# Two woven layers on one core: stores of the turned features on ScalarE's queue, and the last block's feature steps at another pace

## The chip, the core and the metric

The kernel runs on one core of a Trainium2 chip. The core has five engines that each work through their own instructions in order: TensorE (PE in the profile, with PEld for its weight loads), VectorE (DVE), ScalarE (ACT), GpSimdE (POOL) and SyncE (SP). An engine waits for another by semaphores. Transfers (DMAs) are begun by an instruction in the queue of SP or of ScalarE and are then carried out by 16 DMA engines; the instruction that begins one waits, in its queue, for the data that it sends. The metric is the time on the device in microseconds, the median of the runs.

## What is computed

An input x of 2048 rows and 576 columns in fp32 goes through two pairs of layers: linear attention with a learned feature map (32 heads of 18 columns), then an MLP with a squared ReLU and 4608 hidden units. Both use the same weights in both pairs.

```python
def attend(x):                       # on the layer norm of x
    q, k, v = heads(x @ wqkv)
    pq, pk = q @ w_phi, k @ w_phi    # one 18x18 matrix a head
    phi = lambda p: concat([softmax(p), softmax(-p)])
    kv = einsum("bhsf,bhsd->bhfd", phi(pk), v)
    z = einsum("bhsf->bhf", phi(pk))
    num = einsum("bhqf,bhfd->bhqd", phi(pq), kv)
    den = einsum("bhqf,bhf->bhq", phi(pq), z) + 1e-6
    return merge(num / den) @ wo

def mlp(x):                          # on the layer norm of x
    h = relu(x @ w1 + b1)
    return (h * h) @ w2 + b2

for _ in range(2):
    x = x + attend(layernorm(x))
    x = x + mlp(layernorm(x))
```

## The kernel before

Each fp32 operand of a matrix product is split in two parts that TensorE takes at full speed, and a product is three products (high by high, low by high, high by low). The rounding to the high part is ScalarE's work, the difference VectorE's and GpSimdE's.

The 2048 rows are four blocks of 512 rows, and a block is four tiles of 128 rows (t = 0 to 3). The MLP's 4608 hidden units are 36 groups of 128. A group is: the loads of its weights on SP (m_2r, the columns of w1 at L1159 and L244, the rows of w2 at L1161); their rounding on ScalarE (m_2h at L1167, m_2s at L1168 and L1169); the first products on TensorE (m_2ph, 14 matmuls at L1190); Relu and two squares on ScalarE (m_2hr, m_2hb at L1197 to L1199); the second products (m_2acc at L1217 and L1208), which TensorE takes one group behind the first ones. The digit in such a name is the block: m_2 is the MLP of block 2. The trace leaves out the layer, so a_0 and m_0 can be of either.

A layer has an order of its blocks, [3, 2, 0, 1] in the first and [1, 0, 3, 2] in the second. The MLP of order[0] (m_3, then m_1) is woven with the attention of order[1] and with the queries and features of order[2]. The MLP of order[1] (m_2, about 510 to 750 us; m_0, about 1700 to 1950 us) is woven with the rest of order[2]'s attention, then with the whole attention of order[3] (a_1 in the first layer, a_2 in the second), then with the prelude of a pair of MLPs that order[2] and order[3] go through together.

The order of the instructions is set as the program is written, by `weave`: after each step of the MLP (a group has 1 such step) the other side gets `rate` units, and each of its steps costs the units that it names. A smaller cost or a higher rate puts the step earlier. Nothing is sorted later: what is written behind another instruction of the same engine stands behind it in its queue. `held` also places a step behind the MLP's latest square and its low part.

The change touches the features of a block, `g_features`, once each for order[1] and order[2] in `back_first` and for order[3] in `back_second`. Its four tiles go through a pipeline of steps: the parts of the softmax, its exponential, its sums and the products with z, the factors, the scaling, and `turn`. In a round each tile that is under way takes one step, the later steps first, and one more tile begins. `turn` transposes a tile of 128 rows and 1152 columns in squares of 32 on VectorE (L897) and then begins four stores of 144 KB to device memory (a_1ft<-a_1Q1e: block 1, tile 1; L900). When all sixteen stores of a block have landed, `g_out` loads the turned features back (a_1w, L928, in five pieces: 126, 72, 126, 126 and 126 rows), ScalarE rounds each half of a piece (a_1fh, L941), VectorE makes the low part (a_1fl, L942), and TensorE multiplies them (a_1pn, L964). The attention's result is added to x on GpSimdE (L1051) and stored by SP (xm, L1052).

All transfers that SP and ScalarE begin take turns on eight semaphores (DMAHW0 to DMAHW7 in the rows below). A transfer waits in its queue until the one before it on its semaphore has landed.

Of the kernel before, what the change touches and what calls it, by code (L numbers as in the profile page):

```python
# [21 lines left out]
def layers_kernel(  # L22
# [18 lines left out]
    nc = tc.nc  # L41
# [60 lines left out]
    def drain(gen):  # L102
        for _ in gen:
            pass

    def weave(main, other, rate, behind=None):

        due = 0.0
        for _ in main:
            due += rate  # L110
            while due >= 1.0:
                cost = next(other, other)
                if cost is other:
                    break
                due -= cost or 1.0
        with tc.issue_after(dense[behind]) if behind else nullcontext():
            drain(other)

    def pipeline(n, stages, costs):

        for i in range(n + len(stages) - 1):
            for k in reversed(range(len(stages))):
                if 0 <= i - k < n:
                    stages[k](i - k)
                    yield costs[k]

    def paced(gen, cost):
        for own in gen:
            yield own if cost is None else cost
# [510 lines left out]
    def soft_parts(src, name, apart=False):  # L640
        if apart:
            e = sb.tile([P, 2 * D], F32R, tag="hb", name=f"{name}e").bitcast(F32)
            e = e.rearrange("p (s d) -> p s d", s=2)
        else:
            e = sb.tile([P, 2, D], F32, tag="E", name=f"{name}e", bufs=4)
        v = src.rearrange("p (h d) -> p h d", d=DH)
        mm = sb.tile([P, 2, H], F32, tag="mm", name=f"{name}m")
        nc.vector.tensor_reduce(mm[:, 0], v, op=ALU.max, axis=AX.X)
        nc.vector.tensor_reduce(mm[:, 1], v, op=ALU.min, axis=AX.X)
        e4 = e.rearrange("p s (h d) -> p s h d", d=DH)  # L650
        m = mm.unsqueeze(3).to_broadcast([P, 2, H, DH])
        dense["parted"] = nc.vector.tensor_sub(e4[:, 0], v, m[:, 0])
        dense["parted", 1] = nc.gpsimd.tensor_sub(e4[:, 1], m[:, 1], v)
        return e

    def soft_exp(e):
        return nc.scalar.activation(e, e, AF.Exp)

    def soft_sums(e, name):
        r = sb.tile([P, 2, H], F32, tag="r", name=f"{name}r", bufs=4)  # L660
        nc.vector.tensor_reduce(r, e.rearrange("p s (h d) -> p s h d", d=DH), op=ALU.add, axis=AX.X)
        nc.vector.reciprocal(r, r)
        return r
# [142 lines left out]
    def held(gen, keys=("last",)):  # L806

        while True:
            with ExitStack() as behind:
                for key in keys:  # L810
                    behind.enter_context(tc.issue_after(dense[key].ins))
                cost = next(gen, gen)
            if cost is gen:
                return
            yield cost
# [15 lines left out]
    def phi_products(layer, e, name):  # L831
        zb = sums[layer]["zb"]
        ms = [sb.tile([P, D], F32, tag="qk", name=f"{name}{s}", bufs=5) for s in range(2)]
        for s in range(2):
            (nc.gpsimd if s else nc.vector).tensor_mul(ms[s], e[:, s], zb[:, s])
        return ms
# [13 lines left out]
    def phi_scale(e, r, which=(0, 1)):  # L850
        for s in which:
            e3 = e[:, s].rearrange("p (h d) -> p h d", d=DH)
            dense[f"scaled{s}"] = (nc.gpsimd if s else nc.vector).tensor_mul(
                e3, e3, r[:, s].unsqueeze(2).to_broadcast([P, H, DH]))
# [21 lines left out]

        return product, total, factors, scale

    def g_features(layer, raws, ph, name):

        rs, ms = {}, {}

        def start(t):
            ph.append(soft_parts(raws[t], f"{name}Q{t}"))

        def add(t):
            rs[t] = soft_sums(ph[t], f"{name}Q{t}")
            ms[t] = phi_products(layer, ph[t], f"{name}m{t}")

        def factors(t):  # L890
            phi_factors(phi_sums(ms.pop(t), f"{name}u{t}"), rs[t])

        turned[name] = home = dram.tile([2 * D, TB], F32, name=f"{name}ft")

        def turn(t):
            flat = ph[t].rearrange("p s d -> p (s d)")
            nc.vector.transpose(flat, flat)  # L897
            for i in range(NQ):
                at = t * P + 32 * i
                nc.sync.dma_start(home[:, at : at + 32].rearrange("(j f) r -> f j r", f=32),  # L900
                                  flat[32 * i : 32 * i + 32].rearrange("f (j r) -> f j r", r=32))

        yield from held(pipeline(NT, (start, lambda t: soft_exp(ph[t]), add, factors, lambda t: phi_scale(ph[t], rs[t]),
                                      turn), (2.6, 0.4, 3.0, 2.8, 1.2, 1.6)), ("last", "squared"))

    def g_out(layer, b, ph, dst, name, parts=1, pause=None, behind=None, norm=None, mid=None, costs=(None, None), o_first=None):

# [790 lines left out]
            return x  # L1698
        return get

    def g_attend(layer, b, x, raws, dst, name, behind=None, norm=None, mid=(None, None), ph=None):

        if ph is None:
            ph = []
            if raws is None:
                raws = []
                yield from g_queries(layer, b, x, raws, name)
            yield from g_features(layer, raws, ph, name)
        yield 5.0
        if mid[0]:  # L1710
            yield from mid[0]
        yield from g_out(layer, b, ph, dst, name, behind=behind and (behind["last"],), norm=norm, mid=mid[1],
                         costs=(1.0, None if norm else 3.0))
# [108 lines left out]
    for b in range(NB - 1):  # L1822
        norm = g_norm(load_x(b + 1), xT[b + 1], f"n0_{b + 1}")
# [7 lines left out]
    order = [NB - 1, NB - 2] + list(range(NB - 2))  # L1831
    b, prev = order[0], order[1]
    x, xprev = xT[b], xT[prev]
    for layer in range(2):
        ready, raws = barrier(layer, b, prev, x, xprev, kes, vpair, qpair)
        spare["tags"] = []
        early, operands, rows, nxt, keep = [], {}, [], {}, {}
# [7 lines left out]
        def back_second():  # L1845
            yield from g_attend(layer, order[2], None, None, operands, f"a{layer}_{order[2]}", None,
                                g_norm_first, ph=early)
            yield from g_attend(layer, order[3], None, None, operands, f"a{layer}_{order[3]}", None,
                                lambda *a: held(g_norm_second(*a), ("last", "squared")))
            yield from paced(held(prelude, ("last", "squared")), 2.0)  # L1850

        def rows_of(b):
# [75 lines left out]
        back = chained(back_second())  # L1928
# [2 lines left out]
            drain(back)  # L1931
            next(products)

        weave(g_mlp(layer, order[1], nxt, [], f"m{layer}_{order[1]}", None, then), back, 5.0)
        back = iter(()) if layer else chained(back_keys(), True)
        for k, _ in enumerate(products):
            if k == NP - 1:
# [6 lines left out]
        if layer == 0:  # L1944

            prev, b = order[-2], order[-1]
            spare["tags"] = ["acc0", "acc1", "acc2", "acc3", "h"]
            x, xprev, vpair = {}, keep["x"], keep["v"]
# [14 lines left out]
            order = [b, prev] + order[:2]  # L1963
# [22 lines left out]
```

## Time and profile before

| | |
|---|---|
| median of three runs (2436.8, 2439.97, 2958.45) | 2439.97 us |
| the profiled execution | 2442.47 us |
| its span | 2440.8 us |
| TensorE busy | 2412.5 us, 99% |
| VectorE busy | 1560.7 us, 64% |
| ScalarE busy | 1290.9 us, 53% |
| GpSimdE busy | 939.9 us, 39% |
| stores of turned features, number of issues | 96, all on SP |

The shares are averages over stages that differ, so they don't say where a change counts. What matters is where TensorE stands still, and what it then waits for. In the rows of SP the times are those of the instruction that begins a transfer, not of the transfer. A time in brackets behind a row is how long the engine was idle before it, and what ended that.

### The profile page before, as it was taken

Reading aid. Unit: us, or ns where it says so; the run is one execution under the profiler, and the core shown is the slowest. Engines: PE = TensorE matmul, PEld = TensorE weight load, DVE = VectorE, ACT = ScalarE, POOL = GpSimd, SP = SyncE. Lnnn points to the kernel's source line nnn. Section 1 sums busy time; section 2 is a strip of 40 time slices with the busy share of each in tenths; the row PEclk is TensorE's granted clock in tenths of the full one; section 3 lists DMA queues with packets and bytes.
Section 4 is the critical chain, followed back from the end, with each engine's and each line's share of the span. In section 5 each row is a group of like instructions: output and inputs, shape, how many; then the busy total and the mean of one; then the engine's idle time right before and its main releaser. Section 6 shows DMA issues by size and latency. Waiting matters only on the chain. (4 is left out here: it accounts for less than half of the span.)

```text
span 2440.8 us, 41473 instructions
## 1 busy us (share of the span) xinstructions
PE 2412.5 (99%) x14806; PEld 2140.8 (88%) x14806; DVE 1560.7 (64%) x2537; ACT 1290.9 (53%) x2543; POOL 939.9 (39%) x1121
## 2 busy tenths in 40 slices
PE   9999999999999999999999999999998999999999
PEld 8999888888788888888999988888887888888898
DVE  7778848664866655545766788486557675555443
ACT  4344555444446766664433445554455466676643
POOL 4555303222326565542433442032122455565321
PEclk9999999999999999999999999999999999999999
DMA  9124573756654533338753156637667444333364
GB/s 338 64 84 164 163 194 102 168 185 228 151 159 129 162 105 108 112 102 301 254 188 147 59 167 145 173 96 195 194 224 162 130 143 144 119 103 117 110 199 130
DMA packets 370646, 379.40 MB, mean 155 GB/s; under 512 B 142886, under 2 KB 270790, under 8 KB 367878
## 3 DMA queue, kind: packets, MB, share of 16 engines
q1 hardware_dynamic: 369180, 375.37, 51.3%
q8 instruction: 116, 1.90, 0.3%
q10 hardware_dynamic: 1258, 1.37, 0.2%
q14 instruction: 92, 0.75, 0.1%
HBM read 297.22 MB, written 79.41 MB: 154 GB/s over the span
## 5 line engine op out<-in xcount | busy, mean ns | idle before, releaser
L1508 POOL TENSOR_TENSOR m_ps<-m_pr,m_ps 128x128 fp32r<-128x128 f32 x144 | 98.8, 686 | 338.1 <-ACT m_ps L1506 310.9
L1507 DVE TENSOR_TENSOR m_ps<-m_pr,m_ps 128x448 fp32r<-128x448 f32 x144 | 99.8, 693 | 176.1 <-ACT m_ps L1505 176.0
L1550 PE MATMUL m_pacc<-m_ps,m_phb 128*128 128x448 f32 x864 | 185.6, 363 | 0.0
L1550 PEld LDWEIGHTS m_pacc<-m_ps,m_phb 128*128 128x128 f32 x864 | 161.9, 188 | 15.1
L1550 PE MATMUL m_pacacc<-m_ps,m_phc 128*128 128x448 f32 x648 | 147.1, 365 | 0.0
L1505 ACT ACTIVATE m_ps<-m_pr 128x448 fp32r<-128x448 f32 x144 | 82.8, 575 | 115.8 <-issue 66.6
L1550 PEld LDWEIGHTS m_pacacc<-m_ps,m_phc 128*128 128x128 f32 x648 | 119.2, 188 | 7.7
L1190 PE MATMUL m_2ph<-a_2nh,m_2h 128*128 128x512 f32 (+1 forms) x380 | 98.1, 385 | 1.9 <-ACT m_2h L1167 1.7
L1190 PE MATMUL m_0ph<-a_0nh,m_0h 128*128 128x512 f32 (+1 forms) x380 | 97.6, 383 | 1.8 <-ACT m_0h L1167 1.7
L1217 PE MATMUL m_2acc<-m_2s,m_2hb 128*128 128x448 f32 x432 | 95.4, 368 | 2.9 <-ACT m_2s L1168 2.6
L1217 PE MATMUL m_0acc<-m_0s,m_0hb 128*128 128x448 f32 x432 | 95.2, 368 | 2.9 <-ACT m_0s L1168 2.6
L1190 PE MATMUL m_1ph<-t1onh,m_1h 128*128 128x512 f32 (+1 forms) x380 | 95.8, 381 | 0.5 <-ACT m_1hr L1197 0.3
L1190 PE MATMUL m_3ph<-t0onh,m_3h 128*128 128x512 f32 (+1 forms) x380 | 95.7, 381 | 0.2 <-DVE t0onh L534 0.2
L1217 PE MATMUL m_3acc<-m_3s,m_3hb 128*128 128x448 f32 x432 | 93.6, 363 | 0.0
L1217 PE MATMUL m_1acc<-m_1s,m_1hb 128*128 128x448 f32 x432 | 93.5, 363 | 0.0
L1217 PEld LDWEIGHTS m_2acc<-m_2s,m_2hb 128*128 128x128 f32 x432 | 82.0, 191 | 11.7 <-ACT m_2s L1168 3.0
L1217 PEld LDWEIGHTS m_0acc<-m_0s,m_0hb 128*128 128x128 f32 x432 | 81.7, 190 | 11.6 <-ACT m_0s L1168 3.0
L1217 PEld LDWEIGHTS m_3acc<-m_3s,m_3hb 128*128 128x128 f32 x432 | 80.7, 188 | 7.9 <-DVE m_3hb L1200 0.4
L1217 PEld LDWEIGHTS m_1acc<-m_1s,m_1hb 128*128 128x128 f32 x432 | 80.7, 188 | 7.8 <-DVE m_1hb L1200 0.3
L1175 POOL TENSOR_TENSOR m_3s<-m_3r,m_3s 128x128 fp32r<-128x128 f32 x36 | 22.3, 620 | 158.2 <-ACT m_3s L1169 147.0
L1175 POOL TENSOR_TENSOR m_1s<-m_1r,m_1s 128x128 fp32r<-128x128 f32 x36 | 22.0, 612 | 156.7 <-ACT m_1s L1169 139.4
L1190 PEld LDWEIGHTS m_1ph<-t1onh,m_1h 128*128 128x128 f32 x380 | 68.8, 188 | 15.3 <-ACT m_1hr L1197 0.7
(2464 smaller groups left out, 7241.0 us busy)
## 6 DMA issues: line engine op xcount, KB each, us to landing
m_pr<-in_B_w SPq DMA_DIRECT2D x144, 288.0 KB
m_pr<-in_B_w SPq DMA_DIRECT2D x72, 256.0 KB
hd<-m_pu SPq DMA_DIRECT2D x72, 256.0 KB
m_pg<-hd SPq DMA_DIRECT2D x72, 256.0 KB
m_3r<-in_B_w SPq DMA_DIRECT2D x36, 288.0 KB
m_2r<-in_B_w SPq DMA_DIRECT2D x36, 288.0 KB
m_1r<-in_B_w SPq DMA_DIRECT2D x36, 288.0 KB
m_0r<-in_B_w SPq DMA_DIRECT2D x36, 288.0 KB
```

What stands on the lines that cost most here:

```text
L1175: nc.gpsimd.tensor_sub(s2[:, FC + P : FC + 2 * P], r2[:, R:], s2[:, FC : FC + P].bitcast(F32))
L1190: dense["hidden"] = nc.tensor.matmul(ph[:, cols], a, m, start=(k == 0), stop=(k == len(ops) - 1))
L1217: nc.tensor.matmul(acc[t][:, :R], a[:, rows], m, start=(f == 0 and k == 0), stop=(f == NF - 1 and k == 2))
L1505: nc.scalar.activation(s2[:, RO : RO + R], r2[:, :R], AF.Copy)
L1507: nc.vector.tensor_sub(s2[:, RO + R : RO + 2 * R], r2[:, :R], s2[:, RO : RO + R].bitcast(F32))
L1508: nc.gpsimd.tensor_sub(s2[:, FC + P : FC + 2 * P], r2[:, R:], s2[:, FC : FC + P].bitcast(F32))
L1550: nc.tensor.matmul(accs[b][t][:, :R], a[:, rows], m, start=(g == 0 and k == 0), stop=(g == NF - 1 and k == 2))
```

## The change

The four stores of a tile are taken out of `turn` and become a step of their own, `store`, which comes one round of the pipeline later and begins them from ScalarE's queue instead of SP's. The cost of `turn` falls from 1.6 units to 1.4, and `store` costs 0.2. `g_features` gets a `pace` that multiplies all its costs; it is 1.3 for the features of order[3] and 1.0 for the others. The rate at which the MLP of order[1] is woven goes from 5.0 to 5.2.

```diff
-    def g_features(layer, raws, ph, name):
+    def g_features(layer, raws, ph, name, pace=1.0):
...
             nc.vector.transpose(flat, flat)
+
+        def store(t):
+            flat = ph[t].rearrange("p s d -> p (s d)")
             for i in range(NQ):
                 at = t * P + 32 * i
-                nc.sync.dma_start(home[:, at : at + 32].rearrange("(j f) r -> f j r", f=32),
+                nc.scalar.dma_start(home[:, at : at + 32].rearrange("(j f) r -> f j r", f=32),
                                   flat[32 * i : 32 * i + 32].rearrange("f (j r) -> f j r", r=32))
 
+        costs = [pace * cost for cost in (2.6, 0.4, 3.0, 2.8, 1.2, 1.4, 0.2)]
         yield from held(pipeline(NT, (start, lambda t: soft_exp(ph[t]), add, factors, lambda t: phi_scale(ph[t], rs[t]),
-                                      turn), (2.6, 0.4, 3.0, 2.8, 1.2, 1.6)), ("last", "squared"))
+                                      turn, store), costs), ("last", "squared"))
...
             yield from g_attend(layer, order[3], None, None, operands, f"a{layer}_{order[3]}", None,
-                                lambda *a: held(g_norm_second(*a), ("last", "squared")))
+                                lambda *a: held(g_norm_second(*a), ("last", "squared")), pace=1.3)
...
-        weave(g_mlp(layer, order[1], nxt, [], f"m{layer}_{order[1]}", None, then), back, 5.0)
+        weave(g_mlp(layer, order[1], nxt, [], f"m{layer}_{order[1]}", None, then), back, 5.2)
```

In the rows below the number behind a name's group is that of its buffer, and lines behind `g_features` stand 4 further down in the changed kernel (L928 is L932 there, L1161 is L1165).

SP in m_2, where the features of block 1 end. Before:

```order
L1159 DMA m_2r_18_7536<-in_B_w 128x4x128
L244 DMA m_2r_18_7536<-in_B_w 64x128 x2
L900 DMA a_1ft<-a_1Q0e 32x36x32 x4
L900 DMA a_1ft<-a_1Q1e 32x36x32 x4
L1161 DMA m_2r_17_7473<-in_B_w 128x576
L900 DMA a_1ft<-a_1Q2e 32x36x32 x4
L1161 DMA m_2r_18_7537<-in_B_w 128x576
L900 DMA a_1ft<-a_1Q3e 32x36x32 x4
L1159 DMA m_2r_19_7593<-in_B_w 128x4x128
L244 DMA m_2r_19_7593<-in_B_w 64x128 x2
L1161 DMA m_2r_19_7594<-in_B_w 128x576
L928 DMA a_1w_7646<-a_1ft 126x2x512
```

And SP in the changed kernel, up to the same loads of a_1w:

```order
L1165 DMA m_2r_20_7633<-in_B_w 128x576
L1165 DMA m_2r_21_7694<-in_B_w 128x576
L1163 DMA m_2r_22_7756<-in_B_w 128x4x128
L244 DMA m_2r_22_7756<-in_B_w 64x128 x2
L1165 DMA m_2r_22_7757<-in_B_w 128x576
L1163 DMA m_2r_23_7866<-in_B_w 128x4x128
L244 DMA m_2r_23_7866<-in_B_w 64x128 x2
L1165 DMA m_2r_23_7867<-in_B_w 128x576
L932 DMA a_1w_7746<-a_1ft 126x2x512
L932 DMA a_1w_7748<-a_1ft 72x2x512
L932 DMA a_1w_7750<-a_1ft 126x2x512
L932 DMA a_1w_7814<-a_1ft 126x2x512
```

The stores are gone from SP, the weights of groups 17 to 23 are no longer behind any of them, and the loads of a_1w stand behind the weights of group 23 instead of group 19.

ScalarE in m_2 at the same place. Before, from the weights of group 19 to the first halves of a_1fh and the next group's Relu and squares:

```order
L1167 ACTIVATE m_2h_19_7599<-m_2r_19_7593 128x640
L1168 ACTIVATE m_2s_19_7600<-m_2r_19_7594 128x448
L1169 ACTIVATE m_2s_19_7600<-m_2r_19_7594 128x128
L941 ACTIVATE a_1fh_7702<-a_1w_7646 126x512
L941 ACTIVATE a_1fh_7706<-a_1w_7646 126x512
L1167 ACTIVATE m_2h_20_7656<-m_2r_20_7650 128x640
L1197 ACTIVATE m_2hr_7679<-m_2ph_7607,b1t 128x512
L1198 ACTIVATE m_2hb_7680<-m_2hr_7679 128x512
L1199 ACTIVATE m_2hr_7679<-m_2hr_7679 128x512
L1168 ACTIVATE m_2s_20_7657<-m_2r_20_7651 128x448
L1169 ACTIVATE m_2s_20_7657<-m_2r_20_7651 128x128
L941 ACTIVATE a_1fh_7716<-a_1w_7648 72x512
```

And in the changed kernel the last two tiles' stores, with the Relu that follows them:

```order
L1201 ACTIVATE m_2hr_7661<-m_2ph_7591,b1t 128x512
L1171 ACTIVATE m_2h_21_7699<-m_2r_21_7693 128x640
L1202 ACTIVATE m_2hb_7662<-m_2hr_7661 128x512
L1203 ACTIVATE m_2hr_7661<-m_2hr_7661 128x512
L903 DMA a_1ft<-a_1Q2e 32x36x32 x4
L903 DMA a_1ft<-a_1Q3e 32x36x32 x4
L1172 ACTIVATE m_2s_21_7700<-m_2r_21_7694 128x448
L1173 ACTIVATE m_2s_21_7700<-m_2r_21_7694 128x128
L1201 ACTIVATE m_2hr_7722<-m_2ph_7646,b1t 128x512
L1171 ACTIVATE m_2h_22_7762<-m_2r_22_7756 128x640
L1202 ACTIVATE m_2hb_7723<-m_2hr_7722 128x512
L1203 ACTIVATE m_2hr_7722<-m_2hr_7722 128x512
```

Eight stores stand between the squares of one group and the rounding of the weights m_2s_21; the rounding of a_1fh comes behind the group after them.

ScalarE in m_3, with the waits of each instruction, where the features of block 0 (order[2]) are stored in the changed kernel:

```order
L903 DMA a_0ft<-a_0Q1e 32x36x32 [waits DMAHW5_49]
L903 DMA a_0ft<-a_0Q2e 32x36x32 [waits DMAHW7_49,DVE_49]
L903 DMA a_0ft<-a_0Q2e 32x36x32 [waits DMAHW1_49]
L903 DMA a_0ft<-a_0Q2e 32x36x32 [waits DMAHW2_49]
L903 DMA a_0ft<-a_0Q2e 32x36x32 [waits DMAHW3_49]
L1172 ACTIVATE m_3s_32_5553<-m_3r_32_5547 128x448 [waits PE_49,Pool_49]
L1173 ACTIVATE m_3s_32_5553<-m_3r_32_5547 128x128
L1201 ACTIVATE m_3hr_5575<-m_3ph_5498,b1t 128x512
L1171 ACTIVATE m_3h_33_5654<-m_3r_33_5648 128x640
L1202 ACTIVATE m_3hb_5576<-m_3hr_5575 128x512 [waits Activation_49]
L1203 ACTIVATE m_3hr_5575<-m_3hr_5575 128x512 [waits Activation_49]
L903 DMA a_0ft<-a_0Q3e 32x36x32 [waits DMAHW6_49,DVE_49]
```

These stores stood on SP before; here a Relu (m_3hr) stands behind them, and some of them wait for transfers that SP began.

More of the change, by code (lines that the diff above doesn't have):

```diff
@@ L1699, in load_x, with g_attend @@
         return get
-    def g_attend(layer, b, x, raws, dst, name, behind=None, norm=None, mid=(None, None), ph=None):
+    def g_attend(layer, b, x, raws, dst, name, behind=None, norm=None, mid=(None, None), ph=None, pace=1.0):
         if ph is None:
@@ L1707, in g_attend @@
                 yield from g_queries(layer, b, x, raws, name)
-            yield from g_features(layer, raws, ph, name)
+            yield from g_features(layer, raws, ph, name, pace)
         yield 5.0
```

## The prediction

> **What bounds the kernel now.** I read the page first, then the busy time in stretches of 50 us to find where TensorE loses time, then what it waited for there, then the rows of the engines that released it. The page's first part and three of the stretches:
>
> ```profile
> PE 2412.5 (99%) x14806; PEld 2140.8 (88%) x14806; DVE 1560.7 (64%) x2537; ACT 1290.9 (53%) x2543; POOL 939.9 (39%) x1121
> ...
> 400.00:450.00 50.00, 50.00 (x246) 43.88 (x245) 39.82 (x58) 25.80 (x47) 13.98 (x13) 1.00 0.47 107
> 650.00:700.00 50.00, 42.71 (x183) 34.66 (x182) 27.31 (x44) 23.82 (x46) 5.55 (x7) 0.93 0.91 218
> 1850.00:1900.00 50.00, 43.82 (x180) 35.51 (x179) 30.72 (x46) 25.30 (x47) 6.03 (x7) 0.93 0.86 201
> ```
>
> TensorE bounds the kernel: 28.3 us idle in 2440.8. A usual stretch (400 to 450) is full, at clock 1.00. The two others hold 7.3 and 6.2 of the idle time, and the granted clock is 0.93 in them. They are the same place in the two layers: the second woven block (m_2, m_0), where the features of the last block (a_1, a_2) are turned and read back. What TensorE waited for there, m_2's waits and then m_0's (columns: us in total, times, longest):
>
> ```profile
> PE m_2acc L1217 <- ACT m_2s L1168: 2.6, 1, 2.6
> PE a_1pn L964 <- ACT a_1fh L941: 2.0, 1, 2.0
> PE m_2ph L1190 <- ACT m_2h L1167: 1.7, 1, 1.7
> ...
> PE m_0acc L1217 <- ACT m_0s L1168: 2.6, 1, 2.6
> PE m_0ph L1190 <- ACT m_0h L1167: 1.7, 1, 1.7
> PE a_2pn L964 <- ACT a_2fh L941: 1.6, 1, 1.6
> ```
>
> Two of the three waits are for weights (m_2s, m_2h) and one for the turned features (a_1fh). SP's queue in m_2, DMA issues with start and duration, then the wait that holds it, then the sum of 615 to 650 (columns: length, PE, PEld, DVE, ACT, POOL busy):
>
> ```profile
> 646.76 2.33 SPq L900 DMA_DIRECT2D a_1ft<-a_1Q1e  x4
> 649.18 0.59 SPq L1161 DMA_DIRECT2D m_2r<-in_B_w  x1
> ...
> 655.58 3.50 SPq L900 DMA_DIRECT2D a_1ft<-a_1Q3e  x4
> 659.12 0.71 SPq L1159 DMA_DIRECT2D m_2r<-in_B_w  x1
> ...
> 661.86 0.80 SPq L928 DMA_DIRECT2D a_1w<-a_1ft  x2
> ...
> SPq L900 <- DVE a_1Q1e L897: 8.0, 1, 8.0
> ...
> sum 35.00, PE 35.00 PEld 30.39 DVE 34.80 ACT 19.30 POOL 13.96; mean PE 5.00 PEld 4.34 DVE 4.97 ACT 2.76 POOL 1.99
> ```
>
> So the cause is read backwards: VectorE is full (34.80 of 35.00) and turns a_1Q1e late; SP sits 8.0 us before its four stores; the weight loads m_2r stand behind them in the same queue; ScalarE, which must round those weights, is late; TensorE stops.
>
> **The slow clock after each stop.** TensorE rows, m_2 and then m_0 (a bracket is the idle time before the row):
>
> ```profile
> 657.59 4.07 PE L1217 MATMUL m_2acc<-m_2s,m_2hb 128*128 128x448 f32 x11 [0.32 <-DVE m_2s L1174]
> 667.36 2.57 PE L1217 MATMUL m_2acc<-m_2s,m_2hb 128*128 128x448 f32 x12
> 670.47 0.40 PE L964 MATMUL a_1pn<-a_1fh,kbh 126*126 126x512 f32 x1
> 670.70 0.40 PE L964 MATMUL a_1pn<-a_1fh,kbl 126*126 126x512 f32 x1
> ...
> 674.31 0.51 PE L964 MATMUL a_1pn<-a_1fh,kbh 72*128 72x512 f32 x1 [2.01 <-ACT a_1fh L941]
> 678.30 1.09 PE L1190 MATMUL m_2ph<-a_2nl,m_2h 128*128 128x512 f32 x4
> ...
> 1865.24 3.91 PE L1217 MATMUL m_0acc<-m_0s,m_0hb 128*128 128x448 f32 x11 [0.32 <-DVE m_0s L1174]
> 1881.49 0.50 PE L964 MATMUL a_2pn<-a_2fh,kbh 72*128 72x512 f32 x1 [1.64 <-ACT a_2fh L941]
> 1882.77 0.41 PE L1190 MATMUL m_0ph<-a_0nh,m_0h 128*128 128x512 f32 x1
> 1886.65 1.31 PE L1190 MATMUL m_0ph<-a_0nh,m_0h 128*128 128x512 f32 x5
> ...
> 675.00:680.00 5.00, 5.00 (x17) 3.87 (x16) 2.39 (x5) 2.39 (x5) 0.00 (x0) 0.69 1.00 262
> ```
>
> Twelve second-product matmuls take 2.57, so eleven take 2.36; after the first stop they took 4.07 and 3.91: 1.7 and 1.5 us lost. A 512-column matmul starts every 0.23 us (670.47 to 670.70). After the wait for a_1fh ten starts lie between 674.31 and 678.30, 3.99 us in place of 2.3: 1.7 lost, at clock 0.69 in the last row. In m_0 ten starts lie between 1882.77 and 1886.65: 3.88 for 2.3, 1.6 lost.
>
> Loss to be had: m_2 2.6 + 2.0 + 1.7 idle and 1.7 + 1.7 slow = 9.7; m_0 2.6 + 1.7 + 1.6 and 1.5 + 1.6 = 9.0. Sum 18.7 us.
>
> **The change part by part.** *Stores off SP.* Sixteen issues a block leave SP. The m_2r loads then go out as soon as their own buffer is free, and the waits for m_2s and m_2h go with the slow clock behind the first: 2.6 + 1.7 + 1.7 = 6.0 in m_2, 2.6 + 1.7 + 1.5 = 5.8 in m_0.
>
> *Stores on ScalarE.* The price there is bounded by these rows, the issues that ScalarE makes now and SP's of the same stores (ns, least/median/most):
>
> ```profile
> L315 ACTq DMA_DIRECT2D wf<-ff x5: 326/357/502, 11.7 to 30.7; - x5
> L900 SPq DMA_DIRECT2D a_1ft<-a_1Q3e x4: 384/626/1711, 655.6 to 658.4; - x4
> ...
> 641.69 0.69 ACT L1197 ACTIVATE m_2hr<-m_2ph,b1t 128x512 f32<-128x512 f32 x1 [2.36 <-PE m_2ph L1190]
> 642.28 0.73 ACT L1167 ACTIVATE m_2h<-m_2r 128x640 fp32r<-128x640 f32 x1
> 642.91 0.62 ACT L1198 ACTIVATE m_2hb<-m_2hr 128x512 fp32r<-128x512 f32 x1
> 643.56 0.63 ACT L1199 ACTIVATE m_2hr<-m_2hr 128x512 f32<-128x512 f32 x1
> 656.18 0.56 ACT L1168 ACTIVATE m_2s<-m_2r 128x448 fp32r<-128x448 f32 x1
> 656.65 0.29 ACT L1169 ACTIVATE m_2s<-m_2r 128x128 fp32r<-128x128 f32 x1
> ...
> 667.60 1.15 ACT L941 ACTIVATE a_1fh<-a_1w 126x512 fp32r<-126x512 f32 x2 [1.40 <-DMA a_1w<-a_1ft]
> 673.64 0.61 ACT L941 ACTIVATE a_1fh<-a_1w 72x512 fp32r<-72x512 f32 x1
> ```
>
> One issue costs 0.36 to 0.63; I take 0.6, since it is the same transfer. A group's work on ScalarE runs from 641.69 to 644.19 and from 656.18 to 656.94, 2.5 + 0.8 = 3.3 us. TensorE's group is 14 first products, 14 x 0.23 = 3.2, and the second ones, 667.36 to 670.47 = 3.1: 6.3. With four stores ScalarE needs 5.7, which is hidden. In one group stand eight (Q2 and Q3 back to back): 3.3 + 4.8 = 8.1, 1.8 more than TensorE's. What is queued behind is m_2s and the next Relu, and TensorE waits for that. The squares are used only a group later, which covers most of it: 0.5 us a block, 0 to 1.8. The cover elsewhere is ScalarE's idle half (25.80 of 50.00 in the usual stretch), and costs nothing unless a store waits (below).
>
> *One round later, 1.3 times the units, 5.2 a group.* 45.6 units of features become 1.3 x (4 x 11.4) = 59.3; at 5.2 that is 11.4 groups where it was 9.1. VectorE's 34.80 of 35.00 falls to about 0.8 of it, so it has caught up when the stores come; the round between guards the same. The features end 2.3 groups later, and what follows about 1.3: the last steps of the pair's prelude slip to m_2's end, on VectorE, ScalarE and GpSimdE. TensorE's order there stays; 0, with 1 us a layer if a step is late.
>
> *What is late next.* a_1fh. It needs a_1w, which SP loads once all sixteen stores have landed. From the end of group 19's first products (t0): Relu, the next m_2h and two squares 2.7, eight stores 4.8, so 7.5. Now the loads go out 661.86 - 659.08 = 2.8 after SP's last store was issued, an upper end, since SP issued other loads between; a_1w then takes 667.60 - 661.86 = 5.7. ScalarE can begin a_1fh at t0 + 15.4 to 16.0. TensorE comes to a_1pn after two groups and one second product, 2 x 6.3 + 3.1 = t0 + 15.7. So the first piece, half of the 1.15 later, is late by 0.3 to 0.9; the 72-row piece stands in ScalarE's queue behind the Relu, m_2h, two squares and m_2s of the next group (0.7 + 0.7 + 0.6 + 0.6 + 0.8 = 3.4) and TensorE has only 7 x 0.23 = 1.6 to do meanwhile. Together about 3 us, where 2.0 and 1.6 stood, and one slow clock behind it as now, 1.7. That leaves 4.7 a block, 9.4.
>
> The Trainium skill ("TensorE: Matmul & The Clock Gate", section "HAM oscillation — how this bites in real kernels") asks only for no idle gap above some 3.4 us; by it this wait would slow nothing and the sum would be 3.4 better. The trace disagrees: the gap of 2.01 us is followed by clock 0.69.
>
> **Sum.** 18.7 lost now, 9.4 left, 1.0 for the stores: 8.3 less. The profiled execution took 2442.47 (span 2440.8) against a median of 2439.97, 2.5 more. 2442.5 - 8.3 - 2.5 = 2431.7, so 2432.
>
> **The rivals.** *More (20%):* the wait for a_1fh ends with its loads sooner, or costs no clock. For it: the first stores now go out while later features are still worked on, and the loads share SP with less. 3.4 less gives 2428; with no wait at all, 9.4 less, 2422.
>
> *Waits only move (15%):* SP's stop becomes a_1fh's. If VectorE is still late by the 8.0 us, the last store is late, the Relu and m_2s stand behind it on ScalarE, and a block still loses its nine: 2440. Against it: VectorE gets a quarter more time. By the Trainium skill ("DMA: Bandwidth & Descriptors", section "Issuing engines are not separate DMA queues") starting transfers from several engines saves only the sequencer's time for the issue. That would be 2.3 us of 646.76's row, and no change. The trace says otherwise: SP lost 8.0 in a wait, not in issuing.
>
> *Slower (15%):* the stores of the third block (a_0 in m_3, a_3 in m_1) stop ScalarE. The transfers of both queues take turns on eight semaphores, and in m_3 the last store of a_0Q2e and the first of a_0Q3e would wait for SP's stores of xm, which wait for GpSimdE's a_2x. Rows of before, SP, then ScalarE's Relu in that place, then SP's wait one block on:
>
> ```profile
> 457.19 0.43 SPq L1052 DMA_DIRECT2D xm<-a_2x  x1
> 460.21 1.34 SPq L1052 DMA_DIRECT2D xm<-a_2x  x1
> ...
> 459.23 0.69 ACT L1197 ACTIVATE m_3hr<-m_3ph,b1t 128x512 f32<-128x512 f32 x1 [12.58 <-PE m_3ph L1190]
> ...
> SPq L1052 <- POOL a_0x L1051: 13.9, 3, 6.3
> ```
>
> Against it: ScalarE is idle 12.58 us there, longer than eight issues and an xm store need. It decides from the point at which xm comes more than a few microseconds later than at 457.19; late by the 6.3 of the last row, the Relu comes that much later, with 1.7 of slow clock and 1 more for the second store: 9.0 a layer. 2432 + 18 = 2450.
>
> **How the numbers follow.** Forecast 50%, more 20%, moved 15%, slower 15%. The likeliest gives 2432, between 2429 and 2439 on its own bounds (stores 0 to 3.6, the wait 2 to 4 a block, the prelude 0 to 2). With the rivals the range reaches from 2420, where no wait is left at all and the run lies 2 lower by chance, to 2448, which leaves out the worse half of the slower case. Two per cent is 49 us, about what a measurement tells from no change. None of the cases reaches it: within 96%, faster 2%, slower 2%.
>
> **What would show it.** Right: SP has no wait of 8 us before stores, the waits for m_2s and m_2h are gone, VectorE is below 5.00 a stretch in m_2 before the stores, a wait for a_1fh of about 3 us a block stays with a clock near 0.7 to 0.8. Wrong: a wait for Relu's output (m_2hr, m_2hb) or for m_3hr; no stop at all at a_1pn; or a_1fh's wait at 5 us or more.

## The result, and the profile after

The changed kernel takes 2477.27 us against 2440.12 for the kernel before. The ratio, here and below one of means, is 1.0157, with a 95% interval of 1.0144 to 1.0169; it leaves out one execution of the kernel before that took 2958.45. The change makes the kernel slower by 37 us, which is less than two per cent and far outside the range of 2420 to 2448.

The page of the changed kernel, its busy times, and three stretches of 50 us (columns as in the prediction):

```profile
PE 2423.1 (98%) x14806; PEld 2146.8 (87%) x14806; DVE 1564.8 (63%) x2537; ACT 1286.2 (52%) x2543; POOL 941.5 (38%) x1121
...
300.00:350.00 50.00, 44.95 (x238) 39.90 (x237) 15.35 (x24) 18.84 (x38) 3.79 (x5) 0.93 0.74 173
450.00:500.00 50.00, 46.09 (x223) 39.45 (x222) 26.17 (x45) 19.68 (x37) 9.50 (x12) 0.97 0.73 177
650.00:700.00 50.00, 42.00 (x182) 34.55 (x180) 29.53 (x44) 21.66 (x42) 8.15 (x10) 0.97 0.72 165
```

In a span of 2475.9 us TensorE is idle for 52.8 (28.3 before), and its busy time has grown by 10.6, since the same 14806 matmuls ran slower: 24.5 + 10.6 = 35.1, the whole difference of the spans. The stretch of the last block (650 to 700) has lost as much as before, and two stretches of the first woven MLP, which lost 0.7 and 0.2 of their 50 us, now lose 5.1 and 3.9. What TensorE waits for in the whole run:

```profile
PE m_1ph L1194 <- ACT m_1hr L1201: 9.8, 4, 4.4
PE m_3ph L1194 <- ACT m_3hr L1201: 8.9, 4, 3.6
PE m_0ph L1194 <- ACT m_0hr L1201: 7.6, 3, 4.6
PE m_2ph L1194 <- ACT m_2hr L1201: 6.4, 3, 3.4
PE m_ppx L1522 <- DVE m_pu L1654: 4.8, 2, 2.6
...
PE a_1pn L968 <- ACT a_1fh L945: 1.9, 1, 1.9
...
PE a_2pn L968 <- ACT a_2fh L945: 0.4, 1, 0.4
```

The waits for weights (m_2s, m_2h, m_0s, m_0h: 8.6 us before) are gone. In their place stand 32.7 us of waits for the Relu (m_*hr) at all six blocks of features, and 4.8 at the pair's first products. Where the time goes can be read from ScalarE's rows: from the first Relu of an MLP to its last, m_3 takes 262.7 us instead of 249.3 and m_1 263.2 instead of 249.8, while m_2 (293.8 instead of 294.1) and m_0 (293.1 instead of 291.7) hardly move. So 26.7 of the 35.1 us are lost in the first woven MLPs; in the last blocks the new waits only take the place of the old ones. ScalarE in m_2, its activations (ACT) and its issues (ACTq) in one list, and TensorE's first products in the same stretch, with the end of one group's second products (676.25):

```profile
671.73 4.31 ACTq L903 DMA_DIRECT2D a_1ft<-a_1Q1e  x4
677.19 0.58 ACT L1172 ACTIVATE m_2s<-m_2r 128x448 fp32r<-128x448 f32 x1 [4.90 <-DMA a_1ft<-a_1Q1e]
677.88 0.67 ACT L1201 ACTIVATE m_2hr<-m_2ph,b1t 128x512 f32<-128x512 f32 x1
...
679.79 4.16 ACTq L903 DMA_DIRECT2D a_1ft<-a_1Q2e  x4
684.04 3.01 ACTq L903 DMA_DIRECT2D a_1ft<-a_1Q3e  x4
687.84 0.67 ACT L1201 ACTIVATE m_2hr<-m_2ph,b1t 128x512 f32<-128x512 f32 x1
```

```profile
662.60 1.30 PE L1194 MATMUL m_2ph<-a_2nh,m_2h 128*128 128x512 f32 x5
670.54 1.43 PE L1194 MATMUL m_2ph<-a_2nh,m_2h 128*128 128x512 f32 x5 [1.49 <-ACT m_2hr L1201]
676.25 0.86 PE L1212 MATMUL m_2acc<-m_2hb,m_2s 128*128 128x512 f32 x3
678.60 1.43 PE L1194 MATMUL m_2ph<-a_2nh,m_2h 128*128 128x512 f32 x5 [1.49 <-ACT m_2hr L1201]
688.56 2.50 PE L1194 MATMUL m_2ph<-a_2nh,m_2h 128*128 128x512 f32 x5 [3.39 <-ACT m_2hr L1201]
```

Groups with a tile's four stores take 7.9 and 8.1 us instead of 6.3, the group with eight stores takes 10.0. Two things can be seen. Four issues take up to 4.3 us, not 2.4. And the Relu stands behind the rounding of m_2s, which begins only after a further gap: the issues end at 676.04, TensorE's second products at 677.11, and m_2s begins at 677.19.

The gap is a matter of order. In the kernel's text `first(f + 1)`, which rounds m_2s of group f + 1, is called before `square(f)`, the Relu of group f. When the program is built its instructions are put in another order than the text's: in the kernel before, the Relu comes first in every group but an MLP's first, as its rows ahead of the prediction show (m_2hr, then m_2s_20). What stands ahead of the prediction on the order, that nothing is sorted later, is wrong for this. In the changed kernel 18 groups, all at or just behind stores, have m_2s of the next group ahead of the Relu (the rows of ScalarE there: m_2s_21, then m_2hr): groups 11 to 13, 29, 31 and 32 of the first woven MLP, and 18 to 20 of the second, in both layers. Why the build turned just these is not shown. m_2s has two buffers, so m_2s of group f + 1 must wait until TensorE is through the second products of group f - 1. The sum of the first products (m_2ph) has one buffer, so TensorE can't begin the next group's first products until the Relu has read it. With the Relu behind m_2s the two wait for each other in turn. In the groups with four stores shown here this alone sets the time: the issues are through 1.1 us before m_2s may begin.

### The profile page after: what moved, and what is told of

Read it like the earlier page. It is cut to its first block, busy times and chain, and to the rows that moved or that the text cites. A ratio compares the mean times of both kernels' runs of the same rounds, so it can differ in the third digit from the quotient of the medians.

```text
span 2475.9 us, 41515 instructions
## 1 busy us (share of the span) xinstructions
PE 2423.1 (98%) x14806; PEld 2146.8 (87%) x14806; DVE 1564.8 (63%) x2537; ACT 1286.2 (52%) x2543; POOL 941.5 (38%) x1121
## 5 line engine op out<-in xcount | busy, mean ns | idle before, releaser
L1194 PEld LDWEIGHTS m_3ph<-t0onh,m_3h 128*128 128x128 f32 x380 | 70.6, 193 | 25.5 <-ACT m_3hr L1201 10.7
L1194 PEld LDWEIGHTS m_0ph<-a_0nh,m_0h 128*128 128x128 f32 x380 | 69.1, 192 | 22.1 <-ACT m_0hr L1201 8.9
```

Of the source, the lines that this page charges most:

```text
L1194: dense["hidden"] = nc.tensor.matmul(ph[:, cols], a, m, start=(k == 0), stop=(k == len(ops) - 1))
```

## The experiments

The theories: **S**, ScalarE stands still for its stores and the Relu is late; **P**, the pace and the rate; **L**, the semaphores that both queues share. Then, within S: **O**, the turned order; **I**, the time of the issues.

**The stores back on SP**, all else as changed.

```diff
-                nc.scalar.dma_start(home[:, at : at + 32] ...
+                nc.sync.dma_start(home[:, at : at + 32] ...
```

> The changed kernel with one word put back: the stores are begun by SP, still one round later, with the pace of 1.3 and the rate of 5.2. Theory S (ScalarE stands still while it issues the stores, its Relu comes late, and TensorE waits for that): the waits for m_1hr, m_3hr, m_0hr and m_2hr (32.7 us together in the changed kernel) go, and the time falls to 2440 or below, to about 2430 if the later round also frees SP's weight loads. Rival P (the pace and the rate make it slower): it stays within 10 us of 2477. Rival L (transfers of either queue stand behind each other on the shared semaphores): as S, but the weight loads behind SP's stores are late again, so about 2440 to 2450.

Measured: 2438.93, ratio to the kernel before 1.0004 (0.9995 to 1.0014). No wait for a Relu is left, and no group but an MLP's first is turned. The whole loss comes with the queue, but no gain is left either: m_0h (3.8), m_2h (1.9) and the pair (m_ppx, 5.0) are waited for, and SP still stands 5.2 and 3.8 us before the stores of a_1Q1e and a_1Q3e for VectorE's transposes.

**The queue alone**: the kernel before with ScalarE's queue in the step of the transpose.

```diff
-                nc.sync.dma_start(home[:, at : at + 32] ...
+                nc.scalar.dma_start(home[:, at : at + 32] ...
```

> The kernel before with one word changed: the four stores of a tile are begun by ScalarE, in the same step as the transpose, with the old pace and rate. Theory S: at least the loss of the changed kernel, 2475 or more, since in the last block ScalarE also waits for VectorE's late transpose (8.0 us on SP before): 2480 to 2500. Rival P: about 2430 to 2440.

Measured: 2488.86, 1.0206 (1.0189 to 1.0223), with 45.3 us of waits for the Relu. The later round and the pace had softened what the queue does.

**The pace alone**: the kernel before with the pace of 1.3 and the rate of 5.2.

> The kernel before with the pace of 1.3 for the last block's features and the rate of 5.2, and the stores as before on SP in the step of the transpose. Theory S: no wait for a Relu; VectorE is less full in the last block, so SP's wait of 8.0 us before the second tile's stores shrinks to below 3 and with it the waits for m_2s and m_2h; 2425 to 2440. Rival P: 2465 or more.

Measured: 2442.20, 1.0011 (1.0002 to 1.0020), above the range that was expected under S. P falls. The expectation of a gain falls too: SP's wait for the second tile's transpose is 9.4 us, longer than the 8.0 before, so the pace does not bring VectorE's transposes ahead of SP's queue. And the pair's wait is the pace's: m_ppx for m_pu, 4.8 us.

**Whole rows**: the changed kernel, each store as 32 rows of 4608 bytes.

```diff
-                nc.scalar.dma_start(home[:, at : at + 32].rearrange("(j f) r -> f j r", f=32),
-                                  flat[32 * i : 32 * i + 32].rearrange("f (j r) -> f j r", r=32))
+                nc.scalar.dma_start(rows[at : at + 32], flat[32 * i : 32 * i + 32])
```

> The changed kernel, but each store writes its 32 partitions as whole rows of 4608 bytes instead of 1152 pieces of 128 bytes, same bytes, same queue, same places in the order; the turned features then stand in the wrong order in memory, so the output is not the reference's. If it is the small pieces that hold ScalarE (they fill the 16 DMA engines, and the issue waits for room): four issues take about 1.3 to 2.4 us instead of 4.3, the waits for Relu go, and the time falls to 2420 to 2440. If ScalarE is held by waits for other transfers (rival L) or by the mere number of issues: it stays at 2460 or more.

Measured: 2459.75, 1.0086 (1.0071 to 1.0101): between the two expectations, which points to two causes. The issues are short now, about 2 us for four, but the order is still the turned one, and a group with four stores still takes 8.06 us (its m_2s at 666.68 and 674.74), as it did with issues of 4.2 us.

**The Relu first**, in the changed kernel. The rounding is written behind the squares of the group before; the stores stay in their groups on ScalarE.

```diff
             if f + 1 < NF:
-                first(f + 1)
+                first(f + 1, late=True)
             hidden(f, every)
             square(f)
+            for high, low in held_back:
+                with tc.issue_after(dense["squared"].ins):
+                    high()
+                low()
+            held_back.clear()
```

> The changed kernel, with the rounding of the second product's weights (m_2s of group f+1) written behind the Relu and squares of group f, which is the order that ScalarE has in the kernel before in every group; in the changed kernel 18 groups around the stores have it the other way round. The stores stay on ScalarE, in the same groups. Theory O (the turned order is the loss: m_2s must wait for the second products of the group before, so the Relu behind it comes 3.9 us late and a group takes 8.06 us instead of 6.29): the waits for m_1hr, m_3hr, m_0hr and m_2hr (32.7 us) fall below 8, and the time is 2430 to 2445. Rival I (the four issues take 4.3 us of ScalarE, and 4.3 + 3.3 is more than the 6.3 of a group): the waits stay above 20, and the time is 2455 to 2475.

Measured: 2459.57, 1.0083 (1.0068 to 1.0098). The time lies in I's range, and the waits for the Relu, 20.2 us, lie at I's limit of 20. But half the loss and 12.5 us of these waits did go, so neither theory is the whole of it. The rows say which waits are left (ScalarE in m_2, then TensorE in m_3):

```profile
662.59 0.69 ACT L1208 ACTIVATE m_2hr<-m_2ph,b1t 128x512 f32<-128x512 f32 x1 [3.00 <-DVE a_1u L845]
665.79 2.98 ACTq L903 DMA_DIRECT2D a_1ft<-a_1Q1e  x3
668.81 0.69 ACT L1208 ACTIVATE m_2hr<-m_2ph,b1t 128x512 f32<-128x512 f32 x1 [2.93 <-PE m_2ph L1201]
...
671.88 3.26 ACTq L903 DMA_DIRECT2D a_1ft<-a_1Q2e  x3
675.51 3.86 ACTq L903 DMA_DIRECT2D a_1ft<-a_1Q3e  x4
679.42 0.69 ACT L1208 ACTIVATE m_2hr<-m_2ph,b1t 128x512 f32<-128x512 f32 x1 [7.25 <-DMA a_1ft<-a_1Q3e]
...
474.57 1.43 PE L1201 MATMUL m_3ph<-t0onh,m_3h 128*128 128x512 f32 x5 [3.52 <-ACT m_3hr L1208]
```

With the Relu first, this group with four stores keeps its 6.2 us (662.59 to 668.81). The group with eight takes 10.6. The stops of TensorE at the four groups with eight stores are 2.09, 2.57, 1.95 and 3.69 us, half of the 20.2. The other half is in the third block of each layer, where no group has eight: in m_3, for one, the last tile's four stores begin late (469.35) and end at 473.78, just before the Relu that TensorE waits for at 474.57.

**The turned order, without the stores**: the kernel before, its stores on SP, with the Relu of the same 18 groups put behind the next group's m_2s.

```diff
+            late = f in ((11, 12, 13, 29, 31, 32) if rest else (18, 19, 20))
+            with tc.issue_after(dense["rounded", f + 1].ins) if late else nullcontext():
                 nc.scalar.activation(hr, ph, AF.Relu, bias=b1t[:, f : f + 1])
```

> The kernel before, its stores on SP as they were, but with the Relu of 18 groups (11, 12, 13, 29, 31, 32 of the first woven MLP and 18, 19, 20 of the second, in both layers) put behind the rounding of the next group's m_2s, as the changed kernel has it. Theory O: each such group takes 8.06 us instead of 6.29, 18 x 1.77 = 32 us more, less what overlaps with the stops that the kernel before has in groups 18 to 20: 2460 to 2480. Rival I: 2437 to 2445.

Measured: 2470.82, 1.0135 (1.0118 to 1.0151), 32 us more, as O expected; but 18 x 1.77 hit this in part by luck. From first Relu to last, m_3 takes 12.9 us and m_1 17.1 us more than in the kernel before, m_2 2.2 less and m_0 1.7 more: the six groups of the last blocks cost next to nothing beside the stops that were there, and the twelve others come to 30.0, more than 1.77 each. TensorE's rows show the stop of 1.49 us with no store on ScalarE:

```profile
306.14 1.30 PE L1190 MATMUL m_3ph<-t0onh,m_3h 128*128 128x512 f32 x5
314.07 1.45 PE L1190 MATMUL m_3ph<-t0onh,m_3h 128*128 128x512 f32 x5 [1.49 <-ACT m_3hr L1199]
```

**The queue alone, the Relu first.**

> The kernel before with the stores on ScalarE in the step of the transpose (old pace and rate), and with the Relu first as in the run before last. Theory O: of the 49 us that this queue alone had cost, the turned order's 32 or more go: 2440 to 2456, with ScalarE's waits for VectorE's transpose left. Rival I: 2470 or more.

Measured: 2468.50, 1.0121 (1.0106 to 1.0136): 20 of the queue's 50 us go with the order. That is fewer than O expected, and more than I did. TensorE still waits 20.4 us for the Relu and 5.4 for the squares (m_2hb, m_0hb), while ScalarE waits and issues.

**The Relu first, old pace and rate.**

> The changed kernel with the Relu first and with the old pace (1.0) and rate (5.0): stores on ScalarE one round later. The pace alone had moved 4.8 us of waits to the pair's first products (m_ppx for m_pu); here they go. Theory O: 2425 to 2440, the best of the four if VectorE's late transposes do not hold ScalarE; if they do (as in the queue alone), 2440 to 2455. Rival I: 2460 or more.

Measured: 2458.47, 1.0082 (1.0067 to 1.0097), in none of the three ranges and nearest to I's. The time is that of the run with the new pace: the pair's wait is gone, but 25.7 us of waits for the Relu stay in place of 20.2.

**Whole rows and the Relu first.**

> The changed kernel with the Relu first and with whole rows of 4608 bytes in each store (the turned features are in the wrong order in memory, so the output is not the reference's). With the small pieces the same order gives 2460. If the issues last long because of the pieces, the groups with eight stores take little more than a usual one here, and the time is 2435 to 2447 with the waits for Relu below 5; if it is the number of issues or the semaphores, it stays at 2455 or more.

Measured: 2434.12, 0.9980 (0.9971 to 0.9990). With both causes away the waits for the Relu are 4.4 us, and the kernel is 4.6 us faster than the one before. Whole rows shorten the transfers as well as the issues, and so also what waits for a transfer to land. The issues of one tile (ns, least/median/most), here and in the changed kernel:

```profile
L904 ACTq DMA_DIRECT2D a_1ft<-a_1Q2e x4: 308/387/433, 663.4 to 665.4; - x4
```

```profile
L903 ACTq DMA_DIRECT2D a_1ft<-a_1Q2e x4: 309/1155/1422, 679.8 to 682.5; - x4
```

The sum of four issues is the least, the most and twice the median: 1.5 us here, 4.0 there. The six kernels side by side (each was measured beside the kernel before, which took 2438.7 to 2440.1):

| Relu against m_2s | stores on | pieces | us |
|---|---|---|---|
| first | SP | 128 bytes | 2438.7 (before) |
| turned in 18 groups | SP | 128 bytes | 2470.8 |
| first | ScalarE | 128 bytes | 2459.6 |
| turned in 18 groups | ScalarE | 128 bytes | 2477.3 (changed) |
| first | ScalarE | whole rows | 2434.1 |
| turned in 18 groups | ScalarE | whole rows | 2459.8 |

The order costs 32 us without the stores on ScalarE, 18 with them, and 26 with whole rows. Order and issues don't add up, since both delay the same Relu.

**The last tile one group later**, with the Relu first, so that the last two tiles' stores are written a group apart.

```diff
         def store(t):
+            costs[-1] = 5.2 if t == NT - 2 else 0.2 * pace
```

> As the changed kernel with the Relu first (2460), and the last tile's four stores one group of the MLP later, so that no group has eight stores on ScalarE. Theory E (what is left after the order is mended are the groups with eight stores, in which the Relu comes 10.6 us after the one before): the waits for m_3hr, m_1hr, m_0hr and m_2hr fall from 20.2 us to below 6, and the time is 2440 to 2448, the rest being the pair's first products (m_ppx, 5.6 us). Rival F (any stores on ScalarE hold it): 2455 or more.

Measured: 2457.65, 1.0078 (1.0063 to 1.0093). The time is in F's range, but the waits fell as E expected: only 1.2 us of waits for the Relu are among the run's longer ones, where there were 20.2. The time did not follow, since the pause was given to the first two blocks of a layer as well, whose attention is then finished late:

```profile
PE a_2po L1004 <- DVE a_2nl L521: 7.1, 1, 7.1
PE a_0po L1004 <- DVE a_0nl L521: 6.5, 1, 6.5
```

**ScalarE for the last block only**, first with the other blocks' stores on SP one round later and with the same pause, which again reached them.

> Stores on ScalarE for the last block only, one round later, the last tile's one group after that, the Relu first; the other two blocks' stores on SP one round later; old pace and rate. Theory E: the stops in the first woven MLPs go altogether, and the last block loses less than the 18.7 us of the kernel before: 2425 to 2436. Rival F: 2445 or more.

Measured: 2452.45, 1.0060 (1.0045 to 1.0075), again in F's range, and again with a loss elsewhere: the stretches from 450 to 550 us, in which another block ends, lose 5.9 us (0.4 before), and those from 1650 to 1750 lose 5.5 (0.4 before).

**SP one round later, old pace and rate.**

> The stores on SP one round later, with the old pace and rate: the one part of the change that was in no run alone. If the round is what VectorE needed, SP's wait of 8.0 us is below 3 and the time 2428 to 2437; if SP's loads are still held by the stores of 2.3 us and VectorE's lag, 2437 to 2443, as before.

Measured: 2439.86, 1.0003 (0.9994 to 1.0013). The round alone gives nothing: SP's wait for the second tile's transpose is 7.3 us, and TensorE's waits for m_0h and m_2h are 7.0 and 5.3.

**Control: the Relu first in the kernel before.**

> The kernel before with nothing changed but that m_2s is written behind the Relu and squares of the group before, the order that ScalarE has there anyway. If this by itself is worth nothing: 2436 to 2442. If it gains or costs more than 5 us, the split between order and issue has to be made against this kernel instead.

Measured: 2438.07, 0.9999 (0.9990 to 1.0009). The edit itself is worth nothing, so the table above holds.

**The last block alone on ScalarE**, the other blocks untouched: Relu first, one round later, the pause before the last tile.

> The kernel before, other blocks untouched, with the last block's stores on ScalarE, one round later, the last tile's one group after that, the Relu first, old pace and rate. If the loss of 18.7 us in the last block is SP's alone: the waits for m_2s and m_2h go, a_1fh and a little of the Relu stay, and the time is 2430 to 2436. If four issues of 3 to 4 us on ScalarE cost as much as they free: 2437 to 2445.

Measured: 2439.58, 1.0003 (0.9994 to 1.0012). Waits for weights are gone, and others of the same size stand there:

```profile
PE m_2ph L1209 <- ACT m_2hr L1216: 3.7, 3, 1.7
PE m_0ph L1209 <- ACT m_0hr L1216: 3.6, 3, 1.8
PE a_1pn L976 <- ACT a_1fh L953: 2.8, 2, 1.9
```

**The last block alone on GpSimdE's queue.**

> The kernel before, other blocks untouched, with the last block's stores on GpSimdE's queue, one round later, old pace and rate. GpSimdE is busy for 5.55 of the 50 us there, so waiting and issuing cost it nothing: if the loss is SP's, 2427 to 2436. If GpSimdE takes several microseconds to prepare each store, its share of m_2s (the low part of 128 columns) comes late behind them, and TensorE's waits for POOL m_2s give 2440 or more.

Measured: 2447.74, 1.0037 (1.0022 to 1.0051). The time is as expected for the worse case, the reason is not: an issue takes 0.82 us, not several. GpSimdE waits 8.85 us for the last transpose, and its share of m_2s stands behind that. TensorE later waits 5.9 us for m_2s, and what it waits for there are weights that SP begins only at 686.29; whether that follows from GpSimdE's wait is not shown. The rows (a bracket is the idle time of the row's engine):

```profile
669.35 3.25 POOL L907 DMA_DIRECT2D a_1ft<-a_1Q3e  x4 [8.85 <-DVE a_1Q3e L897]
672.62 0.52 POOL L1187 TENSOR_TENSOR m_2s<-m_2r,m_2s 128x128 fp32r<-128x128 f32 x1
...
686.29 1.06 SPq L1173 DMA_DIRECT2D m_2r<-in_B_w  x2
690.03 4.85 PE L1229 MATMUL m_2acc<-m_2s,m_2hb 128*128 128x448 f32 x12 [5.89 <-ACT m_2s L1180]
```

**The last block alone on ScalarE, with a pace.** Three settings of pace and rate.

> The last block alone on ScalarE, one round later, the last tile's stores a group after that, the Relu first, with the pace of 1.3 and the rate of 5.2; the other blocks untouched. If the pace is what the queue needed: the waits for m_0hr and m_2hr (7.3 us with the old pace) go, a_1fh's and the pair's (m_ppx, 3 to 5 us) stay: 2430 to 2437. If the pair takes back what the block gains: 2437 to 2443.

> The same with the pace of 1.15: half as much time for VectorE, and an earlier end of the block. If both ends matter, it lies between the old pace (2439.6) and 1.3, with m_ppx below 2 us: 2432 to 2438; else 2438 to 2442.

> The same with the pace of 1.3 and the rate of 5.5, so that the block and the prelude end half a group earlier than in the kernel before rather than later. If the pair's wait is a matter of the prelude's end: no m_ppx, and 2428 to 2435, the best of all; if VectorE is full again at this rate: 2437 to 2442.

Measured: pace 1.3 and rate 5.2, 2436.39, 0.9984 (0.9975 to 0.9993); 1.15 and 5.2, 2434.63, 0.9979 (0.9970 to 0.9989); 1.3 and 5.5, 2435.48, 0.9981 (0.9972 to 0.9991). All three are faster than the kernel before, by 3.5 to 5.2 us of the 8.3 that were forecast for the change, and they can't be told apart. The first two are in their better range, the third is 0.5 us above its own. So stores of small pieces on ScalarE need not make the kernel slower in the last block of a layer (against F); for the first two blocks no run shows that. What is left in the second of them is the wait that the prediction had named as the next one:

```profile
PE a_2pn L977 <- ACT a_2fh L954: 4.2, 1, 4.2
PE a_1pn L977 <- ACT a_1fh L954: 3.9, 1, 3.9
```

## Why the prediction was wrong

**What bounds the kernel now** was read rightly: TensorE, the last block, SP behind VectorE's transposes. In the changed kernel the waits for m_2s and m_2h went as it said.

**The step that failed** is the cost of "Stores on ScalarE": "The squares are used only a group later, which covers most of it: 0.5 us a block". The sentence ahead of it says rightly that the next Relu is queued behind the stores and that TensorE waits for that. The cover was then taken from the squares, and they are not what TensorE waits for next: it waits for the Relu to empty the one buffer of the first products. "A wait for Relu's output" stood in the prediction only as a sign of being wrong. The cover of a group was never there, so a delay of ScalarE ahead of the Relu reaches TensorE once its 3.1 us of second products are done. The runs put 32.7 us of waits there, where the sum had 1.0; with the stores back on SP there were none.

**Two sizes in it were wrong.** The prices of 0.36 to 0.63 us an issue came from a transfer of other shape and from SP's queue. On ScalarE four took up to 4.3 us where 2.4 were taken, and eight took 7.2 where 4.8 were. And "3.3 us" of work in a group was added up without its order: the order rows of the changed kernel showed the Relu behind the eight stores and behind m_2s, and the sum did not ask what m_2s waits for. The turned order alone costs 32 us.

**"The cover elsewhere is ScalarE's idle half ... and costs nothing unless a store waits"** failed in the same way, and it is the larger part: the four other blocks had no term in the sum. A half idle engine is no cover if what it does is due at a point. At these four blocks, where TensorE had waited for almost nothing, it waits 18.7 us for m_1hr and m_3hr, and their MLPs take 26.7 us longer. The last two blocks' 14.0 us of waits stand where there had been waits before.

**"VectorE's 34.80 of 35.00 falls to about 0.8 of it, so it has caught up when the stores come"** had the right size: from 615 to 650 us VectorE is busy for 29.5 of 35 in the changed kernel. That it has then caught up did not hold for SP's queue: with the pace alone SP still waited 9.4 us. For stores on ScalarE the pace did matter: 2439.6 without it, 2434.6 to 2436.4 with it. (The units are 4 x 11.6, not 4 x 11.4, since the store's 0.2 was left out; the end of the features moves by 2.3 groups all the same.)

**"What is late next. a_1fh"** was right in place. It measured 1.9 and 0.4 in the changed kernel, where 3 were forecast, and 3.9 and 4.2 in the version that has no other wait. **The prelude**, priced at 0 to 1 us a layer, was 4.8 in all.

**The rivals.** The slower one had the right sign and the right engine, at 15%, and the waits that it names are in the trace of the changed kernel, in the third block of both layers. Rows of m_1: ScalarE with its issue times, SP's store of xm, and TensorE.

```profile
1683.57 7.74 ACTq L903 DMA_DIRECT2D a_3ft<-a_3Q2e  x4
L903 ACTq DMA_DIRECT2D a_3ft<-a_3Q2e x4: 309/334/612, 1683.6 to 1691.0; - x4
...
1693.94 0.63 ACT L1203 ACTIVATE m_1hr<-m_1hr 128x512 f32<-128x512 f32 x1
1694.63 0.32 SPq L1056 DMA_DIRECT2D xm<-a_0x  x1
1697.78 4.48 ACTq L903 DMA_DIRECT2D a_3ft<-a_3Q3e  x4
1703.78 2.50 PE L1194 MATMUL m_1ph<-t1onh,m_1h 128*128 128x512 f32 x5 [4.40 <-ACT m_1hr L1201]
```

The four stores of a_3Q2e span 7.74 us, but their issues sum to 1.6. By the trace's semaphores the second waits for weights and the fourth for a store of xm, both begun by SP; a_0Q2e in m_3 spans 7.65 us in the same way. This costs little: TensorE's stops behind them are 0.38 and 0.43 us. The first store of a_3Q3e, a tile that was turned long before, waits until the xm store of 1694.63 has landed, 3.2 us after ScalarE's squares end; in m_3 it is 2.2. TensorE's stops behind these are 4.40 and 3.37 us, where a group with four stores that don't wait has 1.49. So the shared semaphores (theory L) cost some 5 us, an estimate from these stops less 1.49 each; the prediction had priced them at 9.0 a layer. The rest of the loss needs no semaphore: it is at all six blocks, and in m_2 the four issues of 671.73 take 4.2 of the 4.31 us themselves (309/1181/1516 ns).

The transfers of both queues did meet in the same 16 engines, as the Trainium skill ("DMA: Bandwidth & Descriptors", section "Issuing engines are not separate DMA queues") says of transfers started by different engines: in one stretch they took 48.9% and 48.2% (last section). By that page the change would have brought no gain; it does not give the loss.

## What to carry to other kernels

Before a transfer is moved to another engine's queue, look in the order for what will stand behind it there, and which buffer that work has to empty, with how many copies: an engine that is half idle can still be on the path at one point of each round. An issue's price belongs to its shape and to what else is in flight: a row of another queue at another time gave 0.6 us here, and 1.1 was measured. And when instructions are added to an engine, compare the order of the old ones as well: here the build turned two of them round in 18 groups, which is worth 18 to 32 us by itself.

## What was not expected of the hardware

An issue of a store in 128-byte pieces takes longer while other transfers are under way. Transfers in the changed kernel between 671.7 and 676.1 us, in which four stores took 4.31 us to issue (columns: packets, MB, share of the 16 DMA engines):

```profile
q1 hardware_dynamic: 802, 0.60, 48.9%
q10 hardware_dynamic: 2633, 0.33, 48.2%
```

SP's weights (q1) and ScalarE's stores (q10) each take half of the engines, which are full. Before, the same four stores had taken 2.33 us on SP, with the engines 71% busy from 646.7 to 649.2 and no weights issued beside them. It does not take a second queue: on SP, one issue of a_1Q3e, right behind the stores of a_1Q2e and a load of weights, took 1.71. As whole rows the issues of one tile took 0.31 to 0.43 us on ScalarE. On GpSimdE's queue four took 3.25, 0.82 each. That it is the full engines that hold the issue is argued from these rows; no run changed the load of SP alone.

The length of a stop alone does not tell whether the clock slows behind it. Five first products usually take 1.30 us. After both stops of 1.49 us in the changed kernel they took 1.43, after the one of 3.39 us 2.50. But with the Relu first they took 1.43 after a stop of 3.52 us (474.57, clock 1.00 from 474 to 479) and 2.13 after one of 1.95. In the kernel before, a stop of 2.01 us had been enough for a clock of 0.69.
